# The beginning written out by hand, row sums in pairs over a tree of accumulating transfers, and the scaled hidden matrix two tiles at a time

## The chip, the cores and the metric

One core of a Trainium2 chip runs the whole program. The metric is the device time of one execution in microseconds (us). TensorE multiplies, VectorE (DVE) and ScalarE (ACT) work on tiles, GpSimd (POOL) issues transfers and does reductions over partitions, and SyncE (SP) issues most loads. Each engine runs its own instructions strictly in order; semaphores let one wait for another. The profiler's page also shows the clock that TensorE was granted.

## The reference

A block of three parts on x, 2048 rows of 1024 values: modulation rows from a condition vector, Fourier mixing, and an MLP.

```python
mod = (_silu(c) @ w_mod).reshape(c.shape[0], 6, 1, -1)      # c 1x1024, w_mod 1024x6144
sa, ca, ga, sb, cb, gb = (mod[:, 0], ..., mod[:, 5])
h = _layernorm(x, axis=-1) * (1 + ca) + sa
# A: a = h Wd_re^T, b = h Wd_im^T; y = Ws_re a - Ws_im b    (real part of a 2-d DFT)
x = x + ga * _A_ref(h, A_dft_seq_re, A_dft_seq_im, A_dft_hid_re, A_dft_hid_im)
h = _layernorm(x, axis=-1) * (1 + cb) + sb
# B: layernorm, Dense 1024 -> 3584, GELU, Dense 3584 -> 1024
x = x + gb * _B_ref(h, B_w1, B_b1, B_w2, B_b2)
```

## The kernel before, in words

Every float32 operand of a product is split into two float16 halves, a high one (a copy on ACT) and the rest (a subtraction on VectorE); a product is three float16 products of these. The work has five stages on TensorE.

1. `plain1`: 16 steps n of 48 products each. Step n multiplies the normalized x tiles n mod 8 and n mod 8 + 8 with a tile of the sequence DFT matrix (real part for n < 8, imaginary part after). Each step needs both x tiles normalized and split (`x_tasks`, L624 to L630) and the DFT tile split into `cop(n)` (`split_c`, ACT L675 then VectorE L678), which has six places.
2. `winograd1`: the other three column blocks tb = 1 to 3 by a seven-product scheme, 84 operands of 24 products. Operands come from `comb_c` (L710) and `split_c`; some products read sums of x tiles, which `s_tasks` splits, stores to DRAM and `sr_load` fetches (four places `sr`). Results go to `uf`, and `u_tasks` splits them and stores them on POOL's queue through three places `O_US`.
3. `gemm2`: products with the hidden DFT matrix, scaled by the modulation, called D' here.
4. and 5. The two dense layers of the MLP (`gemm3`, `gemm4`).

Beside stages 1 and 2 run two more things. *Row sums*: `row_tasks` makes the rows ca, sa, ga, sb, A0, A1, cb and gb, one at a time. For each, eight tiles of weights (128 x 1024) come through three places, VectorE multiplies each by a column and adds it (L490, L492), and POOL sums the 128 partitions with a `partition_all_reduce` (L501). For ca and sa VectorE then picks columns `cs`, `csa` out of the row and works out scales; A0 and A1 need these. ga, sb, cb, gb and gb times b2 are stored to DRAM as 128 equal rows. *D'*: `d_tasks(n)`, n = 0 to 7, loads two tiles of the hidden DFT matrix in one transfer (L805), scales them (L817, with `d0` of L810), splits them and stores the halves (`dc_d`); the next n loads only when n is done, and the first only when the last row is done.

The order on all engines but TensorE is set by a planner that runs while the program is built. Work is given as tasks with a cost, dependencies and a due time, in streams (`push`). Up to TensorE's planned time, `fill_to` records the task that can start and is due first; a task that a product needs and that isn't yet recorded is forced at that point (`emitted`). A split that is forced stands in its engine's queue as late as can be: "recorded just in time" below. The planner takes a transfer as landed after the time in `LANDS` (2.0 us unless given otherwise). POOL's planned reductions do not hold VectorE. Instructions carry numbers in the order in which they were recorded.

The beginning issues c, then x tiles in pairs with a DFT tile behind each of the first four pairs, 18 products on a constant tile (`idle_pe`), and leaves the rest to the planner.

Of the kernel before, what the change touches and what calls it, by code (L numbers as in the profile page):

```python
# [17 lines left out]
P = 128  # L18
# [18 lines left out]
def kernel(ctx, tc, x, cre, cim, dre, dim, w1, b1, w2, b2, c, wm, out):  # L37
# [63 lines left out]
    O_ERLY, O_LATE = (184, 188, 192, 196), (O_AUX, O_AUX + 4, O_AUX + 8, O_AUX + 12)  # L101
# [20 lines left out]
    def sr(n):  # L122

        return at(O_SR + 4 * (n % 4), 2048, F16).rearrange("p (s a d) -> p s a d", s=2, a=2)
# [68 lines left out]
    row_d = {n: dram.tile([P, D], F32, tag=f"row_{n}", name=f"row_{n}") for n in ("ga", "sb", "cb", "gbb", "gb")}  # L193
# [24 lines left out]
    LAGS = {"w": 2.0, "row": 0.2, "z": 1.0, "s": 0.5, "u": 0.3, "op": 0.4, "comb": 0.3, "ln": 0.2}  # L218

    LANDS = {"dma": 2.0, "st": 4.0, ("st", "d"): 7.0, ("st", "u"): 5.0, ("st", "s"): 4.0, ("st", "z"): 4.0}  # L220
# [237 lines left out]
    cs, csa = mk([P, ND], F32, "cs"), mk([P, ND], F32, "csa")  # L458
    m1 = mk([P, 6], F32, "m1")
    ones = at(O_SO[0], 512)  # L460

    mx = mk([P, 3], F32, "mx")
# [7 lines left out]
    def row_tasks(name, places, after):  # L470

        mrow = at(places[0], 1024)
        src = {"A0": 0, "A1": 1}
        r = []
        for k in range(ND):
            b = at(places[1 + k % 3], 1024)

            def load(k=k, b=b):
                if name in src:
                    sp.dma_start(b, dri[src[name]][:, k, :])  # L480
                else:
                    j = ("sa", "ca", "ga", "sb", "cb", "gb").index(name)
                    sp.dma_start(b, wm[:, k, j * D : (j + 1) * D])

            l = Task("dma", 1.5, load, [("row", name, k - 3)] if k > 2 else [after] if after else [], ("wm", name, k))
            col = csa if name in src else scol

            def mul(k=k, b=b):
                if k == 0:
                    dve.tensor_scalar(mrow, b, col[:, 0:1], None, op0=ALU.mult)  # L490
                else:
                    dve.scalar_tensor_tensor(mrow, b, col[:, k : k + 1], mrow, op0=ALU.mult, op1=ALU.add)  # L492

            deps = [l.key] + ([("row", "sa", "end")] if name in src else [])
            r.append((l, Task("dve", 1.3 if k else 0.7, mul, deps, ("row", name, k))))
        t = [l for l, _ in r[:3]]
        for k in range(ND):
            t.append(r[k][1])
            if k + 3 < ND:
                t.append(r[k + 3][0])  # L500
        s = Task("pool", 7.0, lambda: gp.partition_all_reduce(mrow, mrow, P, RED.add), [("row", name, ND - 1)])  # L501
        end = ("row", name, "end")
        rows = mrow.rearrange("p (k m) -> p k m", k=ND)

        def column(o):

            def f():
                dve.tensor_tensor(rows, rows, ident[:, None, :].to_broadcast([P, ND, P]), op=ALU.mult)

            def g():  # L510
                dve.tensor_reduce(o, rows, axis=AX.X, op=ALU.add)

            return [("dve", 1.25, f), ("dve", 1.25, g)]

        def largest(n):
            dve.tensor_reduce(mx[:, n : n + 1], mrow, axis=AX.X, op=ALU.max, apply_absolute_value=True)

        def scales():
            m, pm, sd, iu = (m1[:, j : j + 1] for j in range(4))
            dve.tensor_reduce(m, mx, axis=AX.X, op=ALU.max)  # L520
            pow2(pm, m)
            dve.reciprocal(sd, pm)
            dve.tensor_scalar(sd, sd, SD, None, op0=ALU.mult)
            dve.tensor_scalar(iu, pm, 2.0**5 / SD, None, op0=ALU.mult)
            dve.tensor_scalar(cs, cs, sd, None, op0=ALU.mult)
            dve.tensor_scalar(m1[:, 4:5], m1[:, 4:5], sd, -1.0, op0=ALU.mult, op1=ALU.mult)
            dve.tensor_scalar(csa, csa, sd, 1.0 / ONE, op0=ALU.mult, op1=ALU.mult)

        def put(n, dep, key=None):
            return Task("st", 0.0, lambda: sp.dma_start(row_d[n][:, :], mrow), [dep], key)  # L530

        def linked(*steps):
            u = chain(*steps)
            u[0].deps = (s.key,)
            u[-1].key = end
            return u

        if name == "ca":

            def first():  # L540
                dve.tensor_copy(m1[:, 4:5], mrow[:, 0:1])

            return t + [s] + linked(
                ("dve", 0.7, lambda: dve.tensor_scalar(mrow, mrow, 1.0, None, op0=ALU.add)),
                ("dve", 1.2, lambda: largest(0)), ("dve", 0.1, first), *column(cs),
            )
        if name == "sa":
            return t + [s] + linked(("dve", 1.2, lambda: largest(1)), *column(csa), ("dve", 1.3, scales))
        if name in src:
            return t + [s, Task("st", 0.0, lambda: sp.dma_start(arow_d[src[name]][:, :], mrow[0:1, :]), [s.key], end)]  # L550

        def keep():
            if name == "ga":
                dve.tensor_scalar(mrow, mrow, m1[:, 3:4], None, op0=ALU.mult)
            elif name == "cb":
                dve.tensor_scalar(mrow, mrow, 1.0, None, op0=ALU.add)

        b = at(places[1], 1024)

        def keep_b2():  # L560
            dve.tensor_tensor(mrow, mrow, b, op=ALU.mult)

        if name == "gb":
            l = Task("dma", 1.5, lambda: sp.dma_start(b, b2[0].partition_broadcast(P)), [s.key])
            p = put("gb", s.key)
            m = Task("dve", 1.3, keep_b2, [l.key, p.key])
            return t + [s, l, p, m, put("gbb", m.key, end)]
        if name == "sb":
            return t + [s, put(name, s.key, end)]
        k_ = Task("dve", 0.9, keep, [s.key] + ([("row", "sa", "end")] if name == "ga" else []))  # L570
        return t + [s, k_, put(name, k_.key, end)]

# [3 lines left out]

    def x_tasks(k):

        st, (mv, cl) = xst[k % 2], xs[k]
        ve, r, a, ss = (cl[:, n, :] for n in range(4))  # L580
        tiles = (k, k + 8)
        t = []
        if k < 2:
            for n, i in enumerate(tiles):
                sv = st[:, n].rearrange("p (h k) -> p h k", h=2)
                for h in range(2):
                    f = lambda sv=sv, h=h, i=i: dve.bn_stats(sv[:, h], xf(i)[:, 512 * h : 512 * h + 512])
                    t.append(Task("dve", 0.7, f, [("x", i)] + ([t[-1].key] if t else [])))
                t.append(Task("dve", 0.2, lambda sv=sv, n=n: dve.bn_aggr(mv[:, n], sv), [t[-1].key]))
            t += chain(("dve", 0.15, lambda: dve.tensor_scalar(ve, mv[:, :, 1], EPS, None, op0=ALU.add)))  # L590
            t[-1].deps = (t[-2].key,)
        else:

            junk = at(O_U, 1024, F16)
            for n, i in enumerate(tiles):
                f = lambda n=n, i=i: act.activation(junk, xf(i), AF.Copy, accum_out=mv[:, n, 0:1])
                t.append(Task("act", 1.35, f, [("x", i)]))
            t.append(Task("dve", 0.15, lambda: dve.tensor_scalar(ss, mv[:, :, 0], -1.0 / D, None, op0=ALU.mult), [t[-1].key]))
            for n, i in enumerate(tiles):
                f = lambda n=n, i=i: act.activation(junk, xf(i), AF.Square, bias=ss[:, n : n + 1], accum_out=mv[:, n, 1:2])  # L600
                t.append(Task("act", 1.35, f, [t[2].key]))

            def var():
                dve.tensor_scalar(ve, mv[:, :, 1], 1.0 / D, EPS, op0=ALU.mult, op1=ALU.add)

            t.append(Task("dve", 0.15, var, [t[-1].key]))
        s = chain(
            ("act", 0.2, lambda: act.activation(r, ve, AF.Sqrt)),
            ("dve", 0.16, lambda: dve.reciprocal(r, r)),
            ("dve", 0.16, lambda: dve.tensor_tensor(a, r, r, op=ALU.mult)),  # L610
            ("dve", 0.16, lambda: dve.tensor_tensor(a, a, ve, op=ALU.mult)),
            ("dve", 0.15, lambda: dve.tensor_scalar(a, a, -0.5, 1.5, op0=ALU.mult, op1=ALU.add)),
            ("dve", 0.2, lambda: dve.scalar_tensor_tensor(r, r, SH, a, op0=ALU.mult, op1=ALU.mult)),
        )
        s[0].deps = (t[-1].key,)
        t += s
        root = t[-1].key
        for n, i in enumerate(tiles):
# [12 lines left out]
            )  # L631
            u[0].deps = (root,)
            u[-1].key = ("h", k, n)
            t += u
        return t

    def s_tasks(k):
# [1335 lines left out]
```

## Time and profile before

| what | us |
|---|---|
| median of 3 runs | 2011.29 (2009.31 to 2011.5) |
| profiled execution, its own time | 2012.6 |
| its span, first to last instruction | 2010.8 |
| TensorE busy | 1943.2 |
| VectorE busy | 1463.0 |
| ACT busy | 843.6 |
| POOL busy | 224.2 |
| start of stage 2 / 3 / 4 on TensorE | 214.1 / 673.8 / 982.5 |

A timeline row reads: start, length, engine, line, operation, output and inputs, count, and in brackets how long the engine stood before it and what ended that. A row of waits reads: who waited for whom, us in total, times, longest. A row of groups ends with busy time and mean length (in ns), then idle time before. "DMA to landing" gives the time from a transfer's issue to its completion, of one line's transfers.

### The profile page before, as it was taken

What the parts mean: (1) busy time and instruction counts of PE and PEld (TensorE: products, weight loads), DVE (VectorE), ACT (ScalarE), POOL (GpSimd) and SP (SyncE); (2) the same over time, 40 slices, a digit from 0 to 9 for tenths busy, and PEclk for the clock granted to TensorE, in tenths of its full rate; (3) what the DMA queues carried; (4) which work ended last, traced back from release to release, by engine and by line L of the source; (5) the groups of instructions that cost most, each with busy time, mean ns of one, the idle gap of its engine ahead of it and who ended that gap; (6) DMA issues with size and microseconds to landing.
All of it is one profiled execution on the core that took longest, in us unless ns stands there. A gap on an engine that the chain in (4) does not pass through costs nothing. (4 is left out here: it accounts for less than half of the span.)

```text
span 2010.8 us, 23625 instructions
## 1 busy us (share of the span) xinstructions
PE 1943.2 (97%) x8978; PEld 882.8 (44%) x8978; DVE 1463.0 (73%) x1854; ACT 843.6 (42%) x1078; POOL 224.2 (11%) x286
## 2 busy tenths in 40 slices
PE   4999999988999999999999999999999999999999
PEld 1444444433444444444444444444444444444444
DVE  4987897788888557877678999989874354553567
ACT  3642423334444335554477476465333323212311
POOL 0123211321111102221110000000000000000000
PEclk7999999999999999999999999999999999999999
DMA  7377778679667977777856464453377433432323
GB/s 272 100 241 267 261 249 307 236 256 326 216 237 249 422 295 263 274 255 265 328 178 214 161 209 157 147 182 143 138 247 224 127 91 95 121 100 74 110 74 84
DMA packets 143114, 411.86 MB, mean 205 GB/s; under 512 B 15956, under 2 KB 15956, under 8 KB 139416
## 3 DMA queue, kind: packets, MB, share of 16 engines
q1 hardware_dynamic: 116280, 319.37, 46.5%
q0 software_dynamic: 26720, 90.98, 12.7%
q8 instruction: 70, 1.15, 0.2%
q14 instruction: 44, 0.36, 0.1%
HBM read 272.39 MB, written 137.90 MB: 204 GB/s over the span
## 5 line engine op out<-in xcount | busy, mean ns | idle before, releaser
L1686 PE MATMUL ps<-arena 128*128 128x512 f16 x2352 | 511.1, 379 | 3.0 <-DVE arena L1732 1.5
L1577 PE MATMUL ps<-arena 128*128 128x512 f16 x2352 | 510.2, 379 | 2.2 <-ACT arena L1599 2.2
L1176 PE MATMUL ps<-arena 128*128 128x512 f16 x2016 | 442.1, 382 | 17.7 <-DVE arena L678 11.5
L1686 PEld LDWEIGHTS <-arena 128*128 128x128 f16 x2352 | 229.9, 98 | 281.7 <-issue 3.9
L1577 PEld LDWEIGHTS <-arena 128*128 128x128 f16 x2352 | 230.2, 98 | 279.4 <-issue 2.5
L1732 DVE SCALAR_TENSOR_TENSOR arena<-ps,i4c,arena 128x1024 f32<-128x1024 f32 x179 | 229.4, 1282 | 144.4 <-PE ps L1686 143.0
L1176 PEld LDWEIGHTS <-arena 128*128 128x128 f16 x2016 | 198.3, 98 | 261.4 <-issue 23.7
L1408 PE MATMUL ps<-arena 128*128 128x512 f16 x1344 | 292.9, 379 | 6.6 <-ACT arena L1424 4.1
L389 ACT ACTIVATE arena<-arena,shc 128x512 f16<-128x512 f32 (+1 forms) x115 | 116.1, 1019 | 277.1 <-PE ps L1686 184.6
L1126 PE MATMUL ps<-arena 128*128 128x512 f16 x768 | 173.8, 390 | 32.8 <-DVE arena L678 23.5
L1408 PEld LDWEIGHTS <-arena 128*128 128x128 f16 x1344 | 131.3, 98 | 163.3 <-issue 4.7
L414 DVE TENSOR_TENSOR arena<-arena 128x512 f32<-128x512 f32 (+1 forms) x228 | 171.3, 754 | 4.1
L401 DVE SCALAR_TENSOR_TENSOR arena<-arena,shc 128x512 f16<-128x512 f32 (+1 forms) x115 | 128.8, 1123 | 38.5 <-ACT arena L389 38.3
L675 ACT ACTIVATE arena<-arena 128x1024 f16<-128x1024 f32 x100 | 102.5, 1049 | 113.9 <-PE ps L1176 56.7
L1603 DVE TENSOR_TENSOR arena<-arena,ps 128x512 f32<-128x512 f32 x84 | 57.6, 686 | 110.6 <-PE ps L1577 107.3
L1126 PEld LDWEIGHTS <-arena 128*128 128x128 f16 x768 | 76.6, 100 | 130.1 <-issue 33.0
L678 DVE SCALAR_TENSOR_TENSOR arena<-arena 128x1024 f16<-128x1024 f32 x100 | 128.8, 1307 | 4.0 <-ACT arena L675 4.0
L1596 ACT ACTIVATE arena<-arena,b1s,i1c 128x512 f32<-128x512 f32 x84 | 68.5, 815 | 136.8 <-DVE arena L1603 136.8
L767 ACT ACTIVATE arena<-arena 128x1024 f16<-128x1024 f32 x56 | 58.1, 1051 | 113.0 <-DMA u<-arena 66.4
L770 DVE TENSOR_TENSOR arena<-arena 128x1024 f16<-128x1024 f32 x56 | 67.6, 1221 | 28.0 <-ACT arena L767 28.0
L389 ACT ACTIVATE arena<-arena,s1c 128x512 f16<-128x512 f32 (+1 forms) x70 | 60.9, 885 | 36.8 <-DVE arena L414 26.0
L401 DVE SCALAR_TENSOR_TENSOR arena<-arena,s1c 128x512 f16<-128x512 f32 (+1 forms) x70 | 66.3, 960 | 10.5 <-ACT arena L389 10.4
(155 smaller groups left out, 1435.0 us busy)
## 6 DMA issues: line engine op xcount, KB each, us to landing
w<-arena SPq DMA_DIRECT2D x64, 512.0 KB, 5.1
arena<-w SPq DMA_DIRECT2D x119, 256.0 KB, 2.8
u<-arena POOLq DMA_DIRECT2D x56, 512.0 KB, 7.2
arena<-u SPq DMA_DIRECT2D x112, 256.0 KB, 4.5
arena<-w SPq DMA_DIRECT2D x56, 512.0 KB, 3.5
arena<-in_wm_dram SPq DMA_DIRECT2D x48, 512.0 KB, 6.0
arena<-s SPq DMA_DIRECT2D x48, 512.0 KB, 6.9
arena<-in_cre_dram SPq DMA_DIRECT2D x32, 512.0 KB, 8.5
```

Source lines behind the costliest of these rows:

```text
L389: act.activation(o[m][0], q(j), AF.Copy, **sc)
L401: dve.scalar_tensor_tensor(o[m][1], q(j), scale, o[m][0], op0=ALU.mult, op1=ALU.subtract)
L414: dve.tensor_tensor(q(d), q(a), q(b), op=op)
L675: h = Task("act", 1.15, lambda: act.activation(o[:, :, 0], s2, AF.Copy, scale=SC), list(deps) + free)
L678: dve.scalar_tensor_tensor(o[:, :, 1], s2, SC, o[:, :, 0], op0=ALU.mult, op1=ALU.subtract)
L1126: pe.matmul(bank_of(d_), hleft(d_, s, kp, a), cop(n)[:, s, b], start=(kp == 0 and s == 0 and a == 0 and b == 0), stop=(kp == 7 and s == 1 ...
L1176: pe.matmul(bank_of(st + ch), left, cop(n)[:, s, b], start=(start and kp == 0 and s == 0 and a == 0 and b == 0), stop=(kp == 3 and s == 1 ...
L1408: pe.matmul(bank_of(bk), up(N)[:, c_, a], dp(n)[:, c_, w], start=(start and ri == 0 and c_ == 0 and i == 0), stop=(ri == 1 and c_ == 3 and ...
L1577: pe.matmul(ps.rearrange("p (k t) -> p k t", k=4), w1c[:, m, s, a, d * P : (d + 1) * P], zc(m)[:, b, :, d, :], start=(start and d == 0 and ...
L1596: act.activation(dst, src, AF.Gelu_apprx_tanh, scale=inv, bias=b1s[:, 2 * p + j : 2 * p + j + 1])
L1686: pe.matmul(t[:, j], hidc[:, c_, m, a, k * P : (k + 1) * P], w2c[:, m, c_, w], start=(start and c_ == 0 and n == 0), stop=(c_ == 1 and n = ...
L1732: lambda: dve.scalar_tensor_tensor(dst, ps[b], inv, dst, op0=ALU.mult, op1=ALU.add), kp[b],
```

## The change: the beginning by hand, rows in pairs, trees of transfers, D' ahead

- *Beginning.* The first x tile comes as two half transfers, then half a DFT tile, the ninth x tile, the other half; c is issued from ACT. `first_pair` writes out every instruction for the first two x tiles and the first DFT tile, half a tile at a time; `x_tasks` gives each of the next three pairs in two parts, one with statistics on VectorE, the other on ACT. There are 19 constant products.
- *Rows in pairs.* `pair_tasks` takes (ca, sa), (ga, sb), (A0, A1), (cb, gb). Loads are a stream of their own through four or five places; the multiplications stay the same, 64 in all. The partitions are summed by seven transfers on POOL's queue, each adding half of the remaining partitions to the other half, the next waiting for the one before. The results, one row each, are stored to DRAM. `cs` and `csa` are loaded from there as columns; only one number per partition is still reduced on POOL (L560).
- *D'.* `d_tasks` loads its two tiles singly, into one of two pairs of places, a step ahead; its splits are due every 32 us (`DGAP`) from 70 us into stage 2 on, ahead of the row pair (cb, gb).
- *Places and due times.* `sr` has three places instead of four, freeing 4 KB a partition; `u` stores have two until number 42, then three; `u_tasks` are due 25 us or more earlier. `LANDS` of a load is 3.5 instead of 2.0, with 4 to 6 for some. The rows come back by broadcast loads.

```diff
-    LAGS = {"w": 2.0, "row": 0.2, ...}
+    LAGS = {"w": 2.0, "row": 0.4, ...}
-    LANDS = {"dma": 2.0, "st": 4.0, ...}
+    LANDS = {"dma": 3.5, "st": 4.0, ...}
...
-    def row_tasks(name, places, after):
...
-        s = Task("pool", 7.0, lambda: gp.partition_all_reduce(mrow, mrow, P, RED.add), [("row", name, ND - 1)])
...
+    def pair_tasks(j, due, free):
...
+        while n:
+            f = lambda n=n: gp.dma_start(both[0:n], both[n : 2 * n], accum_op=ALU.add)
+            t.append(Task("pool", 0.7, f, [last, muls[ND - 1].key], ("tree", j, n)))
+            last = t[-1].key
+            LANDS[last] = 3.0
+            n //= 2
...
+            def get():
+                for name, o in (("ca", cs), ("sa", csa)):
+                    v = row_d[name][0].rearrange("(k p) -> p k", p=P)
+                    sp.dma_start(o, v, allow_slow_non_contiguous=True)
+                sp.dma_start(m1[:, 4:5], row_d["ca"][0][0:1].partition_broadcast(P))
...
+            def largest():
+                dve.tensor_scalar(cs, cs, 1.0, None, op0=ALU.add)
+                dve.tensor_reduce(m, cols, axis=AX.X, op=ALU.max, apply_absolute_value=True)
...
+                "dve", 0.9, lambda: dve.tensor_scalar(r[0], r[0], m1[0:1, 3:4], None, op0=ALU.mult),
+                [last, ("row", "sa", "end")],
...
+    def first_pair():
...
-        return at(O_SR + 4 * (n % 4), 2048, F16)...
+        return at(O_SR + 4 * (n % 3), 2048, F16)...
...
+    U3 = 42
+    def u_place(n):
+        if n < U3:
+            return O_US[n % 2], n - 2
...
-        l = Task("dma", 2.9, lambda: sp.dma_start(b, dri[ri][:, c_::4, :]), [("dd", n - 1)] if n else [("row", "gb", "end")])
+        b = [at(o, 1024) for o in ((AUX[0], AUX[1]) if n % 2 else (60, 216))]
+        dep = ("dd", n - 2) if n > 1 else ("row", "A1", "end") if n else ("row", "A1", ND - 1)
+        for h in (1, 0):
+            f = lambda h=h: sp.dma_start(b[h], dri[ri][:, c_ + 4 * h, :])
+            ls.append(Task("dma", 1.5, f, [dep, ("row", "A0", "end") if n == 1 else ("g1", 15)]))
...
-    for n, name in enumerate(("ca", "sa", "ga")):
-        push("row", "early", row_tasks(name, O_ERLY, last), t_op(6) + 30.0 * n)
-    for n, name in enumerate(("sb", "A0", "A1", "cb", "gb")):
-        push("row", "row", row_tasks(name, O_LATE, last), t_op(16) + 10.0 + 24.0 * n)
-    for n in range(8):
-        push("row", "row", d_tasks(n), t_op(16 + 28) + 24.0 * n)
+    pair_tasks(0, t_op(5), {o: ("op", 2) for o in RING[0]})
+    pair_tasks(1, t_op(9), {**was, AUX[2]: ("op", 6), AUX[3]: ("op", 7)})
+    pair_tasks(2, t_op(16) + 35.0, s_end)
+    for n in range(8):
+        push("row", "row1", d_tasks(n), t_op(16) + 70.0 + DGAP * n)
+    pair_tasks(3, t_op(16) + 90.0 + 8.0 * DGAP, d_end)
```

The order on VectorE at the beginning, before: L624 normalizes the first x tile, L587 takes statistics of the third, L490 multiplies the first tile of row weights, L630 splits the first x tile, L678 the first DFT tile.

```order
L624 TENSOR_SCALAR arena_65<-arena_65,xmv_11_196,xcl_12_197 128x1024
L625 MEMSET arena_65 128x1
L587 BN_STATS xst_10_195<-arena_65 128x6
L490 TENSOR_SCALAR arena_65<-arena_65,scol_188 128x1024
L630 TENSOR_TENSOR arena_65<-arena_65 128x2x512
L678 SCALAR_TENSOR_TENSOR arena_65<-arena_65 128x2x512
```

VectorE at the same place in the changed kernel (L630 is the normalization there, L667 the split of half the DFT tile, L638 of half the x tile, L657 statistics of the second tile):

```order
L630 TENSOR_SCALAR arena_65<-arena_65,xmv_9_196,xcl_10_197 128x512
L632 MEMSET arena_65 128x1
L630 TENSOR_SCALAR arena_65<-arena_65,xmv_9_196,xcl_10_197 128x512
L667 SCALAR_TENSOR_TENSOR arena_65<-arena_65 128x512
L638 TENSOR_TENSOR arena_65<-arena_65 128x512
L657 BN_STATS xst_7_194<-arena_65 128x6 x2
```

No row multiplication stands ahead of the splits any more; the first one (L503) stands some 90 rows further on.

POOL's queue around the first row sums, before (L659 stores the split sums of x tiles, L501 is a reduction):

```order
L659 DMA s_81<-arena_65 128x1024
L659 DMA s_82<-arena_65 128x1024
L659 DMA s_84<-arena_65 128x1024
L659 DMA s_83<-arena_65 128x1024
L501 ISA arena_65<-arena_65 128x1024
```

POOL's queue in the changed kernel (L771 stores the split sums, L902 stores u tiles, L519 is one step of the tree, L526 a put of a finished row):

```order
L519 DMA arena_65<-arena_65 64x2048
L771 DMA s_84<-arena_65 128x1024
L771 DMA s_83<-arena_65 128x1024
L519 DMA arena_65<-arena_65 32x2048
L902 DMA u_6_0_97<-arena_65 128x2048
L902 DMA u_0_0_85<-arena_65 128x2048
L519 DMA arena_65<-arena_65 16x2048
L519 DMA arena_65<-arena_65 8x2048
```

Each step waits for the landing of the one before, and stores stand behind waiting steps.

VectorE where it needs a finished tree (second pair), in the changed kernel: L569 scales the finished row ga, L790 splits DFT operands, L767 and L753 to L756 are for the sums of x tiles.

```order
L755 TENSOR_TENSOR arena_65<-arena_65 128x512
L756 TENSOR_TENSOR arena_65<-arena_65 128x512
L790 SCALAR_TENSOR_TENSOR arena_65<-arena_65 128x2x512 x3
L569 TENSOR_SCALAR arena_65<-arena_65,m_6_193 1x1024
L767 TENSOR_TENSOR arena_65<-arena_65 128x2x512 x2
```

L569 is new in this place: it waits for the seventh step, and three operands are split ahead of it. For the first pair the same holds of L545 (it adds 1 to the loaded columns), which has one operand's split, the thirteenth, behind it and none ahead of need.

More of the change, by code (lines that the diff above doesn't have):

```diff
@@ L481, in load, with mul @@
                 else:
[L482 to L488, printed above, removed]
+                    m = MODS.index(name)
+                    sp.dma_start(b, wm[:, k, m * D : (m + 1) * D])
+            def mul(i=i, k=k, b=b, col=col):
@@ L489, in mul @@
                 if k == 0:
-                    dve.tensor_scalar(mrow, b, col[:, 0:1], None, op0=ALU.mult)
+                    dve.tensor_scalar(rows[i], b, col[:, 0:1], None, op0=ALU.mult)
                 else:
[L492 to L513, printed above, removed]
@@ L571, in row_tasks @@
-        return t + [s, k_, put(name, k_.key, end)]
+                    dve.scalar_tensor_tensor(rows[i], b, col[:, k : k + 1], rows[i], op0=ALU.mult, op1=ALU.add)
+            loads.append(Task("dma", 1.5, load, [used.get(o) or free[o]], ("wm", name, k)))
+            LANDS[loads[-1].key] = 4.0 if j else 6.0
+            deps = [loads[-1].key, ("row", "sa", "end") if name in src else None]
+            if k == 0:
+                deps.append(free.get(place + 4 * i))
+            muls.append(Task("dve", 1.3 if k else 0.75, mul, deps, ("row", name, k)))
@@ new lines, in pair_tasks, with put @@
+            used[o] = muls[-1].key
+        push("wl", f"wl{j}", loads, due)
+        push("row", f"row{j}", muls, due)
+        t, last = [], muls[-1].key
+        n = P // 2
+        while n:
[4 more added lines that the diff above has]
+            n //= 2
+        def put(v, dst, dep, end=None):
+            u = Task("pool", 0.7, lambda: gp.dma_start(dst, v), [dep], end)
+            LANDS[u.key] = 3.0
+            return u
@@ L574 @@
+        push(f"tree{j}", f"row{j}", t, due)
     xst = [mk([P, 2, 12], F32, f"xst{n}") for n in range(2)]
     xs = [(mk([P, 2, 2], F32, f"xmv{n}"), mk([P, 4, 2], F32, f"xcl{n}")) for n in range(8)]
[L577 to L607, printed above, removed]
@@ L1119, in plain1 @@
                 if ri and kp == 7 and s == 0 and d == 0:
[L1120 removed]
+                    need("row0")
+                    emitted(("row", "sb", ND - 1))
                 if n == 0 and s == 0 and 0 < d < 4:
@@ L1382, in f @@
             sp.dma_start(wb(b), x[2 * b : 2 * b + 2].rearrange("r p e -> p r e"))
-        was = [("turn", b - 2, n) for n in range(2)] if b > 1 else [("g1", opn(3, 5, 3))]
+        was = [("turn", b - 2, n) for n in range(2)] if b > 1 else [("g1", opn(3, 5, 3)), ("row", "gb", "end")]
         if b == 1:
```

409 lines of the change are left out of this document (278 added, 131 removed).

## The prediction

> **What bounds the kernel now.** I read the page first: TensorE is busy for nearly the whole span, so a gain can only come from its gaps and from matmuls at a lower clock.
>
> ```profile
> span 2010.8 us, 23625 instructions
> PE 1943.2 (97%) x8978; PEld 882.8 (44%) x8978; DVE 1463.0 (73%) x1854; ACT 843.6 (42%) x1078; POOL 224.2 (11%) x286
> ```
>
> Second, the timeline of TensorE alone: start, length, operation, count, and in brackets the gap before it and what ended it.
>
> ```profile
> 1.49 6.07 PE L468 MATMUL ps<-arena 128*128 128x512 f16 x18 [1.49 <-DVE arena L1443]
> 14.02 1.89 PE L1126 MATMUL ps<-arena 128*128 128x512 f16 x4 [6.46 <-ACT arena L629]
> 36.04 42.55 PE L1126 MATMUL ps<-arena 128*128 128x512 f16 x188 [20.13 <-DVE arena L678]
> 81.25 1.04 PE L1126 MATMUL ps<-arena 128*128 128x512 f16 x2 [2.66 <-ACT arena L629]
> ...
> 202.25 11.99 PE L1126 MATMUL ps<-arena 128*128 128x512 f16 x47 [3.37 <-DVE arena L678]
> ...
> 309.46 98.58 PE L1176 MATMUL ps<-arena 128*128 128x512 f16 x456 [1.76 <-DVE arena L678]
> 410.51 22.35 PE L1176 MATMUL ps<-arena 128*128 128x512 f16 x95 [2.47 <-DVE arena L678]
> 433.94 5.35 PE L1176 MATMUL ps<-arena 128*128 128x512 f16 x24 [1.08 <-DMA arena<-s]
> 441.54 12.44 PE L1176 MATMUL ps<-arena 128*128 128x512 f16 x49 [2.25 <-DMA arena<-s]
> 459.27 151.98 PE L1176 MATMUL ps<-arena 128*128 128x512 f16 x695 [5.30 <-DVE arena L678]
> ```
>
> A warm matmul takes 0.216 us (98.58/456). After a gap of 2.5 us or more the next ones are slower: 47 in 11.99 us is 1.9 us over 47 x 0.216, 95 in 22.35 is 1.8 over, 188 in 42.55 is 1.9 over. So each longer gap costs its length and some 1.9 us. Nearly all gaps lie before 640 us and most end with VectorE (L678, the split of a DFT operand).
>
> Third, the first 40 us on all engines.
>
> ```profile
> 4.65 1.28 DVE L587 BATCH_NORM_STATS2 xst<-arena 128x6 f32<-128x512 f32 x2 [3.21 <-DMA arena<-in_x_dram]
> 6.55 1.29 DVE L587 BATCH_NORM_STATS2 xst<-arena 128x6 f32<-128x512 f32 x2 [0.38 <-DMA arena<-in_x_dram]
> 9.76 1.06 ACT L675 ACTIVATE arena<-arena 128x1024 f16<-128x1024 f32 x1 [5.68 <-DMA arena<-in_cre_dram]
> 10.72 0.19 ACT L608 ACTIVATE xcl<-xcl 128x2 f32<-128x2 f32 x1
> 10.95 0.17 DVE L609 RECIPROCAL xcl<-xcl 128x2 f32<-128x2 f32 x1 [2.66 <-ACT xcl L608]
> 11.94 0.81 DVE L624 TENSOR_SCALAR arena<-arena,xmv,xcl 128x1024 f32<-128x1024 f32 x1
> 14.96 1.06 ACT L596 ACTIVATE arena<-arena 128x1024 f16<-128x1024 f32 x1 [0.99 <-DMA arena<-in_x_dram]
> 22.71 11.36 SPq L483 DMA_DIRECT2D arena<-in_wm_dram  x4
> 32.96 0.75 DVE L490 TENSOR_SCALAR arena<-arena,scol 128x1024 f32<-128x1024 f32 x1 [19.48 <-DMA arena<-in_wm_dram]
> 33.63 1.22 DVE L630 TENSOR_TENSOR arena<-arena 128x1024 f16<-128x1024 f32 x1
> 34.76 1.22 DVE L678 SCALAR_TENSOR_TENSOR arena<-arena 128x1024 f16<-128x1024 f32 x1
> ```
>
> Everything for the first product had landed by 9.76 us. VectorE's queue, however, had a row multiplication (L490) ahead of the two splits the product needs, and its weights, issued behind twenty other loads, landed at 32.9. That queue order alone is the 20.1 us gap.
>
> Fourth, what the row sums do: the groups by line, and VectorE's timeline while one of them runs.
>
> ```profile
> L501 POOL PARTITION_ALL_REDUCE arena<-arena x8 | 59.5, 7434 | 126.7 <-DVE arena L492 126.7
> L641 DVE TENSOR_TENSOR arena<-arena 128x512 f32<-128x512 f32 x8 | 9.8, 1229 | 0.0
> L644 DVE TENSOR_TENSOR arena<-arena 128x512 f32<-128x512 f32 x8 | 5.5, 691 | 0.2
> 72.12 5.03 DVE L641 TENSOR_TENSOR arena<-arena 128x512 f32<-128x512 f32 x1
> 409.23 6.70 DVE L678 SCALAR_TENSOR_TENSOR arena<-arena 128x1024 f16<-128x1024 f32 x2
> DVE arena L554 <- POOL arena L501: 6.0, 1, 6.0
> ```
>
> L641 and L644 are equal work; the one that met the reduction of 71 us took 5.03 instead of 0.69, so VectorE stood 4.3 us. The pair at 409 lost 6.70 - 2 x 1.22 = 4.3, another waited 6.0 outright. At 4.3 for each of eight that is some 34 us of VectorE's time. Two of them (71 to 78, 191 to 198 us) lie right ahead of the gaps of 2.66 and 3.37.
>
> **The change, part by part.** The sum is against the profiled execution's own 2012.6 us, 1.3 above the median of the runs.
>
> *The beginning.* Half-tile loads come first; ahead of the splits stands nothing but the first pair. By bytes, the first half of the DFT operand (after 0.75 MB, between the rows of 4.65 and 6.55, and slower than x by the row of 9.76) lands near 6.3. Then: half a copy 0.6 and a root 0.2 on ACT, four small VectorE steps 0.8, half a normalization 0.45, half a copy 0.6: first product near 9. Its second halves arrive with c near 9.8 and the next x near 11; VectorE's work up to the second operand's split is six statistics at 0.64 to 0.69, some 25 small steps at 0.17, normalizations 2.6 and splits 6.3 (1.22 whole), 17 us from 4.65 on; it ends near 22.5, so TensorE waits about 1.2 + 0.5 inside operand 0, 2 before operand 1 and 2 before operand 2. It reaches operand 3 near 45; before, 36.04 + 140 x 0.216 + 1.9 = 68. Gain 23 (if the waits vanish 27; if x1 is as late as the 14.96 row, ACT's sum of x1, which stands ahead of the second root, holds all by 4 and the waits grow: 16).
>
> *Reductions.* All eight L501 go (one of a single column stays). The two gaps behind them with 1.9 of slow clock each: 10. Of the other six, 26 us of VectorE's time, the gaps of 1.76 and 2.47 (+1.9) can profit: 4 of 6. Together 14, from 9 (these only move) to 16. By the Trainium skill, SBUF — State Buffer, "SBUF: two separate sides", the pair of ports that VectorE and GpSimd share is an exclusive lock held for the whole instruction; by it all 59.5 us would come back instead of 34. The 4.3 of a 7 us instruction decides against the full figure.
>
> *D' and the loads.* The multiplications stay 64 at 1.28. D' loads come two tiles ahead. Before, VectorE stood in line for them, ahead of splits:
>
> ```profile
> 442.59 0.75 DVE L810 TENSOR_SCALAR arena<-arena,m 128x1024 f32<-128x1024 f32 x1 [4.07 <-DMA arena<-in_dre_dram]
> 601.07 2.48 DVE L817 SCALAR_TENSOR_TENSOR arena<-arena,cs 128x1024 f32<-128x1024 f32 x2 [5.58 <-DMA arena<-in_dim_dram]
> ```
>
> The gaps there are 1.08 + 2.25 + 5.30 with 3.8 of slow clock; those near 612 add about 5. Of these 17 I take 10 (0 to 17), because the same VectorE work stands elsewhere.
>
> *The trees.* New: 4 x 7 accumulating transfers on POOL's queue, each waiting for the one before, plus nine puts. No such chain is in the trace. Bounds:
>
> ```profile
> cc<-in_c_dram SPq DMA_DIRECT2D x1, 4.0 KB, 1.6
> DMA to landing us min/median/max: 5.9/10.0/13.0
> DMA to landing us min/median/max: 5.5/5.5/5.6
> DMA to landing us min/median/max: 2.9/7.2/14.3
> ```
>
> The rows are 4 KB alone, the accumulating 512 KB of L1785 and of L1760, and the u stores of L772. Low: seven times 1.6, and 3.9 (5.5 - 1.6) for the first step's bytes, halved at each step, 7.8 together: 19. High: 4.3 more for each step, as the u stores show (7.2 - 2.9): 49. I take the middle, 33: small steps stand behind other traffic, but move little. VectorE waits in line twice. At L545 the chain is 33 + 3 (puts) + 5 (column loads), 41, against 24 full and 12 half instructions, 38 us, ahead of it: 3 (0 to 21), felt by TensorE, since the splits are recorded just in time there: 4 with clock. At L569: 33 against 21, 12 late, covered by three operands (72 products, 15.5 us); I charge 3. POOL's s stores queue behind these waits, and ACT and the first s loads behind them: 3. Sum +10 (0 to 30). By the Trainium skill, DMA: Bandwidth & Descriptors, "Anatomy of one DMA", a transfer takes 2.0 us plus bytes over 436 GB/s: an estimate of 16 us a tree, and this term would be near 0.
>
> *Smaller rings.* u stores have two places instead of three, s loads three instead of four. Before, with three:
>
> ```profile
> ACT arena L767 <- DMA u<-arena: 66.4, 18, 12.3
> DMA to landing us min/median/max: 3.8/6.9/14.1
> DVE arena L1281 <- DMA arena<-row_ga: 13.5, 1, 13.5
> ```
>
> An s load now has two operands, 10.4 us, to land in; the median 6.9 fits, the 14.1 (second row) doesn't. ACT is busy 42%, so most waits hide: +3 (0 to 10). Broadcast loads instead of loads of 512 KB rows: nothing. VectorE stood 13.5 us for them before (third row) while TensorE had products whose loads were earlier; without that cover a slower load would cost its own delay, a few us.
>
> Sum: -23 - 14 - 10 + 10 + 3 = -34: 1978.6 profiled, 1977 as a median. Its own range is 1966 to 1990.
>
> **The rivals.**
> 1. *Nearly free of gaps.* The trees take the low end and no wait reaches TensorE: -23 - 14 - 17 + 0 + 0 = -54, 1957. For it: VectorE regains 34 us. Against: the same 64 multiplications in the same stage.
> 2. *VectorE is the bound.* The early pairs pack it fuller in the first 300 us; each tree's wait then goes to TensorE whole: the low gains of 16, 9 and 5 against 15 for trees and 3: -12, 1999. For it: splits 12 to 15 and 26 to 35 are recorded only when their product is due, as was the split that ended the gap before 202.25 and those before 441 to 459. Against: the lost 34 us of VectorE give room.
> 3. *Slower.* One mechanism: VectorE stands at L545 and L569 for the trees. Wait grows with the step; at the 13.0 of L1785's worst, a tree is 91 us, and L545 waits 61, L569 70 less 15: 116 lost against 44 gained, 2083. It decides at a mean step of 8 us (56 a tree: 26 + 20 = the gains). Against: steps halve in size.
> 4. *No change* would need gains and waits to cancel within 4 us.
>
> **Chances.** Forecast 0.56, rival 1 0.18, rival 2 0.18, rival 3 0.05, rival 4 0.03. What a measurement of this kernel can tell from no change is about 0.2%, 4 us. Cases 1, 2 and the forecast are faster: 0.92; same 0.03; slower 0.05. The range takes in rivals 1 and 2 up to about 1955 and 2001.
>
> **What would show it.** The first long run of L1268 starts near 9, with gaps under 3 us up to 40. No VectorE instruction of 5 us or more before 420. In the waits, VectorE's L545 and L569 with under 15 us each; POOL's tree steps 2 to 8 us apart. If TensorE waits over 5 us near operand 13 or 24, the trees cost more than I take; if the first product starts after 14, the beginning is mis-sized.

## The result: 23.7 us faster, ten less than forecast, and the profile after

The changed kernel takes 1987.65 us in the median (1987.0 to 1989.65), the kernel before 2011.39 us in the runs beside it. The ratio is 0.9885, with an interval of 0.9868 to 0.9902. In a second comparison it was 0.9897 (0.9883 to 0.9911). So the gain is 20 to 24 us, where the prediction said 34. The profiled execution took 1989.65 us, 2.0 more than the median.

The page's first lines, and then the timeline of TensorE (start, length, operation, count, and in brackets the gap ahead and what ended it):

```profile
span 1987.7 us, 23757 instructions
PE 1939.7 (98%) x8979; PEld 882.1 (44%) x8979; DVE 1437.1 (72%) x1872; ACT 842.2 (42%) x1081; POOL 190.9 (10%) x316
```

```profile
9.32 6.23 PE L1268 MATMUL ps<-arena 128*128 128x512 f16 x26 [0.90 <-ACT arena L637]
15.78 5.14 PE L1268 MATMUL ps<-arena 128*128 128x512 f16 x23 [0.23 <-DVE arena L638]
22.37 10.52 PE L1268 MATMUL ps<-arena 128*128 128x512 f16 x48 [1.46 <-DVE arena L790]
33.29 104.08 PE L1268 MATMUL ps<-arena 128*128 128x512 f16 x480 [0.40 <-DVE arena L790]
149.91 12.37 PE L1268 MATMUL ps<-arena 128*128 128x512 f16 x48 [12.55 <-DVE arena L790]
165.92 31.13 PE L1268 MATMUL ps<-arena 128*128 128x512 f16 x143 [3.64 <-DVE arena L790]
...
257.30 18.45 PE L1320 MATMUL ps<-arena 128*128 128x512 f16 x72 [5.75 <-DVE arena L790]
...
356.49 295.43 PE L1320 MATMUL ps<-arena 128*128 128x512 f16 x1368 [2.13 <-DMA arena<-s]
```

Three things are to be read from it. The beginning is what was forecast: the first product at 9.32, and operand 3, the fourth, at 33.29 + 48 x 0.217 = 43.7 (operands are counted from 0). Most of the stretch in which D' is made (its multiplications run from 299 to 501 us) lies in one row without a gap, 1368 products in 295.43 us or 0.216 each. Between the two there is a gap that the kernel before did not have: 12.55 us ahead of operand 12, 3.64 ahead of operand 13, and several smaller ones up to 356, the largest 5.75 ahead of operand 26.

Milestones of each profile, in us (stage 2 is the first L1176/L1320 product, stage 3 the first of L1408/L1552; operand 3 is worked out from the products ahead of it):

| kernel | operand 3 | stage 2 | stage 3 | span |
|---|---|---|---|---|
| before | 68 | 214.1 | 673.8 | 2010.8 |
| changed | 43.7 | 196.9 | 651.8 | 1987.7 |

So 24 us were won by operand 3, only 17 of them are left at stage 2, and 22 at stage 3. What comes after stage 3 is alike.

Where the gap comes from is read on all engines from 117 to 150 us. SPq is SyncE's queue of DMA issues, POOL L519 a tree step, L526 a put.

```profile
117.94 24.13 SPq L499 DMA_DIRECT2D arena<-in_wm_dram  x3
137.23 0.79 POOL L519 DMA_DIRECT2D arena<-arena  x1 [1.95 <-DMA arena<-arena]
140.01 0.52 POOL L526 DMA_DIRECT2D row_ca<-arena  x1 [1.98 <-DMA arena<-arena]
142.12 0.96 SPq L815 DMA_DIRECT2D arena<-in_cre_dram  x2
143.13 0.51 SPq L539 DMA_DIRECT2D cols<-row_ca  x1
147.44 1.29 DVE L505 SCALAR_TENSOR_TENSOR arena<-arena,scol 128x1024 f32<-128x1024 f32 x1 [8.41 <-DMA arena<-in_wm_dram]
148.64 1.22 DVE L790 SCALAR_TENSOR_TENSOR arena<-arena 128x1024 f16<-128x1024 f32 x1
```

SyncE issued three loads of weights for the second pair in 24 us. It was standing, and every load behind it stood with it. VectorE then stood 8.41 us at the multiplication (L505) that needs one of these weights, and the split of operand 12 (L790) was next in its queue. SyncE's own waits between 95 and 185 us say for what it stood (in all, times, longest):

```profile
SPq L499 <- DMA arena<-arena: 13.9, 1, 13.9
SPq L499 <- DMA row_ca<-arena: 8.1, 1, 8.1
```

13.9 us were for the tree (arena to arena) and 8.1 for its puts, most of these still for the tree's end, since the first put was issued only at 140.01. The second pair loads through places 184 and 188, which the first tree's rows occupy until they are put. VectorE's waits for a tree, up to 660 us, were of another size:

```profile
DVE arena L578 <- DMA arena<-arena: 16.6, 1, 16.6
DVE arena L569 <- DMA arena<-arena: 5.2, 1, 5.2
DVE cols L545 <- DMA cols<-row_ca: 0.6, 1, 0.6
```

Only 0.6 us at L545; the 16.6 at L578 (the fourth pair) lies inside the row without gaps and cost TensorE nothing.

### The profile page after: what moved, and what is told of

It reads as the page before. It is cut to its first block, busy times and chain, and to the rows that moved or that the text cites. A ratio compares the mean times of both kernels' runs of the same rounds, so it can differ in the third digit from the quotient of the medians.

```text
span 1987.7 us, 23757 instructions
## 1 busy us (share of the span) xinstructions
PE 1939.7 (98%) x8979; PEld 882.1 (44%) x8979; DVE 1437.1 (72%) x1872; ACT 842.2 (42%) x1081; POOL 190.9 (10%) x316
## 5 line engine op out<-in xcount | busy, mean ns | idle before, releaser
L1320 PE MATMUL ps<-arena 128*128 128x512 f16 x2016 | 439.5, 381 | 15.5 <-DVE arena L790 10.5
L1320 PEld LDWEIGHTS <-arena 128*128 128x128 f16 x2016 | 197.7, 98 | 257.2 <-issue 15.9
L1552 PE MATMUL ps<-arena 128*128 128x512 f16 x1344 | 294.0, 381 | 2.7 <-ACT arena L1568 2.7
L1552 PEld LDWEIGHTS <-arena 128*128 128x128 f16 x1344 | 131.9, 98 | 160.0 <-issue 5.3
L790 DVE SCALAR_TENSOR_TENSOR arena<-arena 128x1024 f16<-128x1024 f32 x99 | 118.8, 1217 | 8.0 <-ACT arena L787 7.8
L900 DVE TENSOR_TENSOR arena<-arena 128x1024 f16<-128x1024 f32 x56 | 67.6, 1218 | 19.8 <-ACT arena L897 19.8
L402 DVE SCALAR_TENSOR_TENSOR arena<-arena,s1c 128x512 f16<-128x512 f32 (+1 forms) x70 | 66.4, 959 | 10.1 <-ACT arena L390 10.1
```

The costliest lines, as they stand in the source:

```text
L402: dve.scalar_tensor_tensor(o[m][1], q(j), scale, o[m][0], op0=ALU.mult, op1=ALU.subtract)
L790: dve.scalar_tensor_tensor(o[:, :, 1], s2, SC, o[:, :, 0], op0=ALU.mult, op1=ALU.subtract)
L1320: pe.matmul(bank_of(st + ch), left, cop(n)[:, s, b], start=(start and kp == 0 and s == 0 and a == 0 and b == 0), stop=(kp == 3 and s == 1 ...
L1552: pe.matmul(bank_of(bk), up(N)[:, c_, a], dp(n)[:, c_, w], start=(start and ri == 0 and c_ == 0 and i == 0), stop=(ri == 1 and c_ == 3 and ...
```

## The experiments

The theory at the start was: the first pair's end comes later than the planner assumes (it reckons 3 us for a tree step to land, 3 for a put, 6 for the column loads; the steps took 5.1 in the median), and what is queued in order behind it is late. Its rivals were: VectorE is simply short of time between 100 and 300 us, or the trees as such are dear. The same theory had to show, too, which of the forecast's terms was off.

**The changed kernel again.**

> The changed kernel once more, unedited, as the measure for the runs beside it on the same chip: a ratio of 0.987 to 0.990 to the kernel before, and the gaps before operands 12 and 13 as in its first profile (12.55 and 3.64 us).

Measured 1989.35 us, ratio 0.9897, gaps of 12.70 and 3.55 us, stage 3 at 652.2. The gap is not an accident of one execution.

**The beginning alone**, in the kernel before:

```diff
-    last = None
+    last = ("op", 2)
     for n, name in enumerate(("ca", "sa", "ga")):
         push("row", "early", row_tasks(name, O_ERLY, last), t_op(6) + 30.0 * n)
```

> The kernel before, with one word changed: the loads of the first row wait for the split of operand 2, so that its multiplication (L490) no longer stands ahead of the first product's splits. Theory A (queue order alone makes the gap of 20.1 us): the long run of L1126 starts near 17 instead of 36, operand 3 is reached near 50 instead of 68, and 14 to 20 us are gained: 1991 to 1997. Theory B (loads or the chain of statistics would have held the product anyway): the run starts after 28 and less than 8 us are gained: over 2003.

1998.27 us, ratio 0.9948 (0.9936 to 0.9961): a gain of 10, between the two ranges. The timeline explains it:

```profile
14.98 157.30 PE L1126 MATMUL ps<-arena 128*128 128x512 f16 x717 [0.88 <-DVE arena L678]
182.95 12.34 PE L1126 MATMUL ps<-arena 128*128 128x512 f16 x47 [10.67 <-DVE arena L678]
```

The queue order was the cause of the gap of 20.13: with one dependency changed the run starts at 14.98, and operand 3 is reached near 47, 21 us earlier. So the mechanism of theory A is right, and its gain too large: 10.67 us were given back ahead of operand 15, behind row work: VectorE stood 3.44 us for weights there, and a reduction held one of its instructions for 5.02 us. Time won early by TensorE is kept only if the splits further on are ready earlier too.

**The places of the second pair.**

```diff
-        [(192, 196)[q % 2] if q < 6 else (192, 196, 184, 188)[q % 4] for q in range(16)],
+        [(192, 196)[q % 2] for q in range(16)],
```

> The changed kernel, with the weights of the second pair loaded through two places (192, 196) only, not through the two that the first tree's end frees. Theory A (SyncE stands for the tree at a load of the second pair, and every load behind it is late): SyncE's wait of 24 us is gone, the gaps of 12.55 and 3.64 before operands 12 and 13 shrink to under 3 together, stage 2 starts near 185 instead of 197, 10 to 15 us less than the changed kernel: 1973 to 1978. Theory B (SyncE would stand at the column loads L539 just the same, and VectorE at L545): the gap only changes its place, 1984 to 1990.

1988.78 us, ratio 0.9899 (0.9886 to 0.9911): theory B, the gap changes its place. SyncE no longer waits for the tree at a load of weights, but then at the column loads (L539), and the loads behind those are late instead:

```profile
145.22 13.14 PE L1268 MATMUL ps<-arena 128*128 128x512 f16 x48 [8.40 <-DVE arena L790]
167.51 32.75 PE L1268 MATMUL ps<-arena 128*128 128x512 f16 x143 [9.14 <-DVE arena L790]
SPq L539 <- DMA row_ca<-arena: 10.5, 1, 10.5
```

So the shared places were not the root; taking away one stand in an in-order queue moved it to the next.

**The planner's numbers.** The first run tells it 5 us for a tree step, 7 for a put and 10.5 for the column loads; the second also 8 us for the stores of s and u, the third 6; the fourth changes the tree step alone. The 5 and the 10.5 are near what the changed kernel's trace has (medians of 5.1 and 10.1); the 7 is near the longest landing of a put there (1.6 in the median, 7.3 at most), so for most puts there the 3 was not short.

```diff
-            LANDS[last] = 3.0
+            LANDS[last] = 5.0
...
-            LANDS[u.key] = 3.0
+            LANDS[u.key] = 7.0
...
-            LANDS[u[0].key] = 6.0
+            LANDS[u[0].key] = 10.5
```

For the stores the change is in one line, `("st", "u"): 5.0, ("st", "s"): 4.0`, where both become 8.0 or 6.0.

> The changed kernel, with the planner told what was measured: 5 us for a tree step instead of 3, 7 for a put instead of 3, 10.5 for the column loads instead of 6. Nothing else is edited; it only changes what is recorded ahead of what. Theory A (the first pair's end is recorded too early, so SyncE and VectorE stand for it ahead of splits that are just in time): the gaps before operands 12 and 13 shrink to under 6 us together, stage 3 starts 8 to 16 us earlier than in the changed kernel (651.8): 1971 to 1980. Theory B (between 100 and 300 us VectorE and the DMA engines have too little time in any order): the gaps only move, stage 3 starts between 648 and 656: 1984 to 1992.

> The run with measured landing times, and the s and u stores also told at 8 us (4 and 5 before; measured 6.0 and 5.9 in the median, 10 to 11 at most). Theory A (ACT's splits of s and u stand for stores that land late, with VectorE's splits behind them): the gaps between 234 and 303 us, 13 us in the changed kernel, shrink by half, 3 to 8 us less than with the measured tree alone. Theory B (the stores' lateness is hidden or only moves): within 3 us of that run.

> The run with measured landing times of the trees, and the s and u stores told at 6 us, their measured median, instead of 4 and 5 (8 for both cost 26 us more than leaving them). Theory A (8 was too late a number for u: the last splits of u fall so late that the first norm of stage 3 waits 20.4 us; at the median this does not happen, and the gaps of stage 2 shrink): 1963 to 1969. Theory B (any later number for the stores brings that wait, in parts): 1975 to 1995.

> The changed kernel with one number changed: the planner is told 5 us for a tree step instead of 3; puts and column loads stay at 3 and 6. Theory A (it is the tree's length that the planner had wrong): nearly all of the 20 us, 1968 to 1974. Theory B (it is the end behind the tree, puts of 7 us and column loads of 10, at which SyncE and VectorE stand): less than half, 1980 to 1988.

| kernel | us | ratio | stage 2 | stage 3 |
|---|---|---|---|---|
| changed | 1987.65 | 0.9885 (0.9868 to 0.9902) | 196.9 | 651.8 |
| tree 5, put 7, columns 10.5 | 1969.31 | 0.9799 (0.9786 to 0.9813) | 182.9 | 635.8 |
| the same, s and u stores 8 | 1995.41 | 0.9936 (0.9923 to 0.9950) | 181.1 | 631.5 |
| the same, s and u stores 6 | 1974.36 | 0.9825 (0.9805 to 0.9846) | 182.8 | 644.1 |
| tree 5 alone | 1963.83 | 0.9768 (0.9746 to 0.9790) | 182.1 | 632.1 |

One number in the planner, and no instruction more or less on TensorE, is worth another 24 to 26 us: 0.9768 against 0.9885 and 0.9897. Theory A of the first and the fourth run is right in kind, and both times lie below its ranges (by 2 and 4 us). The put's and the columns' numbers were not needed: with them the time is 1969.31, without them 1963.83. The tree itself became no faster. In the run with the tree number alone it takes from 100.46 to the put at 146.10, 46 us, in the changed kernel 40; yet TensorE waits 3.35 us ahead of operand 12 instead of 12.55:

```profile
100.46 0.94 POOL L519 DMA_DIRECT2D arena<-arena  x1
146.10 0.51 POOL L526 DMA_DIRECT2D row_ca<-arena  x1 [2.13 <-DMA arena<-arena]
140.87 41.38 PE L1268 MATMUL ps<-arena 128*128 128x512 f16 x191 [3.35 <-DVE arena L790]
187.42 68.99 PE L1320 MATMUL ps<-arena 128*128 128x512 f16 x312 [4.95 <-DVE arena L790]
140.85 4.14 SPq L801 DMA_DIRECT2D arena<-in_cim_dram  x2
149.56 0.34 SPq L499 DMA_DIRECT2D arena<-in_wm_dram  x1
SPq L499 <- DMA row_ca<-arena: 3.8, 1, 3.8
SPq L499 <- DMA arena<-arena: 0.6, 1, 0.6
```

SyncE's 13.9 and 8.1 have become 0.6 and 3.8, because loads that other work needs (L801, tiles of the DFT matrix) are now recorded ahead of those that stand for the tree (L499). The rival that VectorE is simply short of time does not hold here. From 100 to 152 us, the changed kernel first, then the tree at 5 us, VectorE (the third of the five engines) was busy 33.23 and 41.30 us: it had the time, and stood.

```profile
100.00:152.00 52.00, 39.45 (x180) 17.53 (x178) 33.23 (x34) 11.32 (x12) 15.01 (x24) 0.88 0.78 252
100.00:152.00 52.00, 48.65 (x226) 22.00 (x225) 41.30 (x42) 18.54 (x19) 19.16 (x31) 1.00 0.89 296
```

More truth in the planner was not always better. With 8 us for the stores stage 3 starts earliest of all five, and then one wait in it loses more than was won; the time is 26 us above the run without the stores' numbers, which neither theory had:

```profile
789.10 1.97 PE L1454 MATMUL ps<-ident,arena 128*128 128x128 f32 x8 [20.41 <-ACT arena L1437]
```

What I wrote ahead of the run with 6 us as the reason (the last u splits too late) is wrong: the last of them, L900, is at 663.3 with 8 us and at 683.0 in the changed kernel. With 6 us neither theory came out: 1974.4 lies between their ranges, 5 us above the run without it, with no such wait. Why the order of stage 3 breaks with 8 us was not followed further. No value for the tree but 3 and 5 was run.

**Reductions in place of the trees**, with the rows still in pairs:

```diff
-        n = P // 2
-        while n:
-            f = lambda n=n: gp.dma_start(both[0:n], both[n : 2 * n], accum_op=ALU.add)
...
+        for i in range(2):
+            f = lambda i=i: gp.partition_all_reduce(rows[i], rows[i], P, RED.add)
+            t.append(Task("pool", 7.0, f, [muls[ND - 1 + i * ND].key, last], ("tree", j, i)))
+            last = t[-1].key
```

The second of the three runs also has put 7 and columns 10.5, as above; the third has instead one line behind the loop, `LANDS[last] = 28.0`, so that the planner puts off what follows the sum.

> The changed kernel with its rows in pairs, but each row summed by the GpSimd reduction of before (two per pair, 7.4 us each) in place of seven accumulating transfers. Theory A (the length of the tree, 40 us against 15, is what opens the gaps before operands 12, 13 and 26): those gaps go, and of the reductions' lock about 14 us come back at most: 1973 to 1985. Theory B (the tree is paid for by the freed VectorE, as the prediction's terms of -14 and +10 say): 1990 to 2001.

> The changed kernel with the GpSimd reduction of before in place of each tree (two per pair, 7.4 us each), and the planner told 7 us for a put and 10.5 for the column loads. To be held against the run with trees and measured landing times (1969.3 us, ratio 0.980). Theory A (what the trees cost and the reductions cost is small; the order made the 20 us): within 5 us of it, 1964 to 1974. Theory B (the prediction's term: 34 us of VectorE's time behind the reductions are worth 9 to 16 us to TensorE): 1978 to 1986. Theory C (a pair's sum in 15 us instead of 45 frees the places and the queues earlier): under 1964.

> The run with two GpSimd reductions per pair in place of the trees, and one number more: the planner is told that the second one lands 28 us late, so that what follows a pair's sum is put off to 42 us after the rows, as with the trees at 5 us a step (1963.8 us, ratio 0.977). The sums themselves are there after 15 us. Theory A (what gains is only that the first pair's end and the second pair are put off behind the splits; the sum's own means costs the same either way): within 6 us of the run with trees, 1960 to 1970. Theory B (the reductions hold VectorE for 4 to 5 us each, eight times, in stretches where splits are just in time): 10 to 25 us above it, 1974 to 1989.

| after a pair's sum | trees | reductions |
|---|---|---|
| recorded early | 1987.65, 0.9885 (0.9868 to 0.9902) | 1984.43, 0.9878 (0.9865 to 0.9891) |
| put off to some 40 us in the plan | 1963.83, 0.9768 (0.9746 to 0.9790) | 1979.90, 0.9853 (0.9837 to 0.9870) |

The run with reductions, put 7 and columns 10.5 stands at 1987.12, 0.9889 (0.9872 to 0.9906), 1 us above the range of its theory B; there too what follows the sum is recorded early, so it does not show B's reason. The first of the three fell into the range of theory A by its time, but not for A's reason: its gap ahead of operand 12 is longer, not gone.

```profile
150.64 43.44 PE L1265 MATMUL ps<-arena 128*128 128x512 f16 x191 [13.59 <-DVE arena L787]
130.93 0.39 SPq L536 DMA_DIRECT2D cols<-row_ca  x1
138.02 1.28 DVE L505 SCALAR_TENSOR_TENSOR arena<-arena,scol 128x1024 f32<-128x1024 f32 x1 [3.57 <-DMA arena<-in_wm_dram]
```

With a sum of 15 us instead of 40, SyncE still stands for the put until 130.93 (its issue before was at 120.74), and VectorE for the weights behind it; then row work stands ahead of the split of operand 12. So the length of the tree was not what opened the gap; what follows the sum stood too early in the queues in either case. The table separates the two. Putting it off is worth 24 us with trees and some 5 (1 to 9) with reductions. With what follows put off, trees are worth 0.0085 or 17 us more than reductions. There the reductions show on VectorE, in the last run, which came out as its theory B (an instruction of L753's shape takes 0.69, one of L765's 1.22):

```profile
99.67 5.75 DVE L765 TENSOR_TENSOR arena<-arena 128x1024 f16<-128x1024 f32 x1 [0.47 <-ACT arena L762]
106.79 5.17 DVE L753 TENSOR_TENSOR arena<-arena 128x512 f32<-128x512 f32 x1
```

The busy time of each engine from 100 to 640 us, reductions first, then trees, both put off (PE, PEld, DVE, ACT, POOL):

```profile
100.00:640.00 540.00, 515.41 (x2350) 231.37 (x2349) 467.51 (x415) 202.84 (x211) 129.92 (x150) 0.98 0.76 270
```

```profile
100.00:640.00 540.00, 525.60 (x2418) 237.10 (x2417) 437.44 (x419) 209.51 (x218) 103.07 (x174) 0.99 0.83 286
```

VectorE is busy 30 us longer for about the same instructions (415 and 419), and TensorE does 68 products fewer in that time, 14.7 us at 0.216. How much of this is VectorE's time itself, and how much the order, is not separated: the planner does not know that a reduction holds VectorE, and no run told it.

**D' through one pair of places, and four places for s.** First the early loads of D' are undone; then, on top, the loads of s get their fourth place back (place 60, which D' no longer uses; the b2 row moves from there to 216, and the third place for u starts after the row gb).

```diff
-        b = [at(o, 1024) for o in ((AUX[0], AUX[1]) if n % 2 else (60, 216))]
+        b = [at(o, 1024) for o in (AUX[0], AUX[1])]
...
-        dep = ("dd", n - 2) if n > 1 else ("row", "A1", "end") if n else ("row", "A1", ND - 1)
+        dep = ("dd", n - 1) if n else ("row", "A1", "end")
```

```diff
-        return at(O_SR + 4 * (n % 3), 2048, F16).rearrange("p (s a d) -> p s a d", s=2, a=2)
+        return at(O_SR + 4 * (n % 4), 2048, F16).rearrange("p (s a d) -> p s a d", s=2, a=2)
...
-        if n > 2:
-            was = [("gs", n - 3)]
+        if n > 3:
+            was = [("gs", n - 4)]
```

> The changed kernel with D' loaded through one pair of places, each tile after the one before it is done, as before the change. Theory A (the early loads are what keeps stage 2 free of gaps from 356 to 652 us; the prediction's term of -10): gaps return near the D' multiplications, 5 to 12 us more than the changed kernel: 1993 to 2000. Theory B (there VectorE simply has less to do at that time, since the rows come earlier): within 3 us of the changed kernel, 1985 to 1991.

> The changed kernel with D' loaded through one pair of places, and four places for the loads of s again instead of three. To be held against the run with one pair of places alone (1996 us, ratio 0.994). Theory A (the prediction's term for the smaller rings, +3): 2 to 6 us less than that run, and TensorE's wait for s loads, 4.9 us in the changed kernel, gone. Theory B (three places are enough): within 2 us of it.

Undoing the early loads costs: 1996.08, 0.9940 (0.9924 to 0.9956) against 0.9885 and 0.9897, theory A. The row without gaps breaks up from 436 to 599 us:

```profile
436.32 10.52 PE L1320 MATMUL ps<-arena 128*128 128x512 f16 x48 [2.30 <-DVE arena L790]
...
598.05 0.38 PE L1320 MATMUL ps<-arena 128*128 128x512 f16 x1 [1.50 <-ACT arena L787]
```

The profile shows less of it than the times: stage 3 starts at 656.1, 4 us later than in the changed kernel, since some small gaps before 356 went away, TensorE's waits for s loads among them. The price is 4 us by the profile and 9 to 11 by the ratios.

With four places for s: 1990.14, 0.9905 (0.9891 to 0.9920), 7 us less than the run before it by the ratios, with an uncertainty of some 4; that is in theory A's direction, but the profiles do not show A's mechanism. TensorE's waits for s loads, in the changed kernel

```profile
PE ps L1320 <- DMA arena<-s: 4.9, 3, 2.1
```

are gone with four places, but they were gone already in the run with one pair of places for D' and three for s. Stage 2, in which these loads are used, starts 2.6 us earlier than there (197.8 against 200.4), and stage 3 only 1.1 us earlier (654.9). What three places for s cost is not shown.

## Why the prediction was right in direction and ten short

*What bounds the kernel* was read right: the gains and losses are gaps on TensorE, and most of them end with a split of VectorE. Exceptions are the waits for s loads (4.9 us) and the 20.41 us in stage 3, which ACT ended.

*The beginning* (-23): right. Operand 3 came at 43.7 (45 forecast, 68 before), 24 us. The waits in it are 0.23, 1.46 and 0.40, where I had 1.7, 2 and 2. What the step left out is that this gain has to survive the next just-in-time split: alone it was worth 10.

*Reductions* (-14, 9 to 16): right in kind, while the size depends on the order. Where what follows the sum is put off in both, trees in place of reductions are worth 17 us (12 to 23), and VectorE gets back 30 us, against the 34 worked out from 4.3 each. In the order of the changed kernel the same exchange is worth nothing (0.9885 and 0.9897 with trees, 0.9878 with reductions), where -14 and +10 made -4.

The Trainium skill says, in SBUF — State Buffer, "SBUF: two separate sides", that the lock is held for the whole instruction. Here the two reductions are on record at 6.08 and 6.06 us and VectorE lost 5.75 - 1.22 = 4.5 and 5.17 - 0.69 = 4.5: as in the kernel before, less than the whole.

*D' and the loads* (-10, 0 to 17): right. The gaps behind 409 us and near 612 went, and undoing the early loads costs 4 to 11.

*Smaller rings* (+3, 0 to 10): open. The fourth place for s gained 7 us by the ratios and 1 in the profile, without the mechanism showing. The third u place was not tried by itself.

*The trees* (+10, 0 to 30): this is the step that failed. As the changed kernel stands, what is recorded behind them costs 24 to 26 us more than with the tree planned at 5 us (0.9768 against 0.9885 and 0.9897), inside the bounds but far over the value taken. Three parts of the step are to be told apart. The tree's length was forecast at 33 (the middle of 19 and 49 is 34), and the four trees took 35 to 41, the first one 40. The places were wrong: I charged 4 at L545, 3 at L569 and 3 for the stores, and the waits were 0.6 and 5.2 (covered, as forecast); what the stores cost was not measured. The place where it was paid was missing: SyncE's queue, where the second pair's loads stand for the first tree's places (and the column loads stand, where those places are not used). The working listed what is queued behind the waiting instructions on VectorE and POOL, and not on SyncE, though the code of the changed kernel puts loads of weights there, into places that the first tree frees. And the planner's 3 us per step stood in the code, 7 x 3.7 = 26 us with the issues, beside a forecast of 33: that the order would be built on a shorter tree than the one forecast was to be seen.

Put together, with -24 (at operand 3), -17, -4 to -11, +24 to +26 and 0 to +7, the measured sizes make between -28 and -12, and -23.7 was measured. They were measured in different orders, so this is no proof of the parts. The time lies inside the stated range of 1966 to 1990, near its slow end; that is owed to the width of the range, since the trees' wait was put in the wrong queue.

*The rivals.* Rival 1 (1957) is close to what the run with the tree's number changed reached, 1963.8. Its condition was "no wait reaches TensorE"; that run still has gaps of 3.35 and 4.95 us. Rival 2 (VectorE is the bound; its sum took 5 for D', whose bound was 0) holds in one stretch. From 234 to 257 us VectorE is busy 22.82 of 23 us and TensorE 15.70, with the gap of 5.75 at its end:

```profile
234.00:257.00 23.00, 15.70 (x72) 7.02 (x72) 22.82 (x20) 6.11 (x6) 1.61 (x3) 0.98 0.97 380
```

With the tree planned at 5 us that gap is gone, so VectorE's time need not be the bound there. Rival 3 (L545 and L569 stand for long) did not happen.

*What would show it* answered well: the first run at 9.3 with gaps of 0.2 to 1.5 up to 40, L545 and L569 under 15 us, no single VectorE instruction of 5 us or more before 420, and TensorE waiting over 5 us near operands 13 and 24 (ahead of 12 and 26), which I had named as the sign of trees that cost more than I take. The tree steps were issued 3.3 to 10.2 us apart, where I had 2 to 8.

## What to carry to other kernels

A planner's latency is a decision about the order: when an operation is replaced by a slower one, its number has to be looked at again, or what is queued in order behind it may be recorded too early, and here one such number was worth as much as the whole change. A measured number is where to begin, not the answer. For the tree it gained 24 us; longer numbers for put and columns beside it gained nothing, the stores' measured median lost 5, and with reductions a number far over the true one gained 5. So each is to be run. Before a new wait is priced, list what stands behind it on every in-order queue, that of the load issues as well as the engines', and follow each place that the waiting work keeps occupied. And a gain early in a kernel with just-in-time work is worth only what the next late operand leaves of it.

## What the runs showed of the hardware that was not expected

A step of an accumulating transfer from partitions to partitions stays slow when it is small. In the four trees of the changed kernel, from one issue to the next, the 512 KB step took 6.7 to 10.2 us, those of 16 to 128 KB still 3.3 to 8.5, and the last, of 8 KB, 2.8 to 2.9 (to the put behind it). The 28 steps landed in:

```profile
DMA to landing us min/median/max: 2.4/5.1/9.9
```

By the Trainium skill, DMA: Bandwidth & Descriptors, "Anatomy of one DMA", 2.0 us and the bytes over 436 GB/s made an estimate of 16 us for a tree; the trace has 35 to 41.

The column loads (1024 single elements of 4 bytes each, L539) landed twice as late as the 5 us forecast:

```profile
DMA to landing us min/median/max: 10.0/10.1/10.2
```

After a gap of about 3.5 us the next products are sometimes slow and sometimes not. In the changed kernel, 143 products after 3.64 us took 31.13 (0.3 over 143 x 0.216); in its second execution the same 143, after 3.55 us, took 32.71, 1.8 over:

```profile
165.75 32.71 PE L1268 MATMUL ps<-arena 128*128 128x512 f16 x143 [3.55 <-DVE arena L790]
```

So the 1.9 us that the prediction charged for every longer gap is no fixed price: it is 0.3 here, and in the run with two places for the second pair the 48 products after 8.40 us took 13.14, 2.8 over.
